# The input columns of a token pair: three full transposes and a stacked remainder, in place of doubled columns

## The chip, the cores and the metric

One core of a Trainium2 chip runs the kernel. The metric is device time in microseconds (us) of one execution; lower is better. Five engines work side by side, each through its own queue in order: TensorE (PE), VectorE (DVE), ScalarE (ACT), GpSimd (POOL) and SyncE (SP), which here issues nearly all transfers.

## What is computed

Each of 33280 tokens has 192 features in 8 heads. A softmax over 7 taps per head weighs the token's own and six earlier rows; the weighted sum is the input of a layer with 1024 hidden units.

```python
    w = exp(weight_gen - max); w = w / (sum(w) + 1e-09)
    out = np.einsum('bshk,bskhg->bshg', w, x_unf)      # 7 taps
    ...
    h = x @ w_in                                        # 192 -> 1024
    e = np.exp(h - h_max)
    solu = h * e / (sum(e) + 1e-09)
    ln = (solu - mu) / np.sqrt(var + 1e-06) * g_ln
    return (ln @ w_out).astype(np.float32)              # 1024 -> 192
```

## The kernel before

A tile is 128 tokens, one on each partition; there are 260 tiles, worked in pairs and in groups of four. Chunks of 4, 8 and then 16 tiles are loaded together (x in four transfers, the weights of the taps in one).

POOL forms the products of a group of four with the taps (L178) and adds them down to three terms (L446, L447, into `half`, two buffers). Before the first group of a chunk it scales the taps (L158 subtracts the maximum, L172 multiplies by the reciprocal that DVE makes at L170). DVE adds the three terms for two tiles at a time (`last_sum`, L464) into `a`. There each tile has 256 columns: its 192, and the last 64 a second time, copied by ACT once per group (`copy_columns`, L468). The first four tiles (`whole`) skip the additions on POOL: PE sums their seven products while it transposes, and DVE sums only the last 64 columns.

For a pair PE transposes four blocks of 128 columns in f32 into one PSUM tile `pa`, the only one of its kind (`transpose_x`, L486): for each tile columns 0 to 127, and columns 128 to 191 doubled. ACT copies `pa` to f16 (`high_x`, L494). PE subtracts that copy from `pa` with `minus` (`subtract_high`, L501, two matmuls of 256 columns; the second leaves the upper 64 rows of the doubled block whole), and ACT copies what is left (`low_x`, L508). So `x_lo[:, 1]` holds the high part of the last 64 features on 64 partitions and the low part on the other 64.

The first product of a tile (`first_product`, L522, here mm1) takes ten matmuls of 512 columns: high times `wa_hi` and `wa_lo`, low times `wa_hi`, and the stacked block times `wb_hi` and `wb_lo`, where `wb` has the last 64 rows of w_in twice. It writes one of three PSUM tiles `h`. DVE takes the maximum (L537), ACT the exponential (L544), DVE the product (L550), ACT the squares (L557) and the high f16 half (L564), DVE the low half (L568). When L557 and L568 of a tile are done, its `h` is free for the tile three later. SP transposes both halves by a transfer (L576), and PE forms the second product (L617, here mm2, 24 matmuls of 192 columns), six tiles behind mm1. ACT scales it (L628), and SP stores four tiles at once (L632).

The order on every engine is not written out. `plan` lists each step with a busy time, what it waits for and slack; `issue_order` walks that list and picks, on the engine that is free first, the step with the lowest key, made of the tile number and a number per step in `URGENCY`, among those that are ready within `PATIENCE`.

Of the kernel before, what the change touches and what calls it, by code (L numbers as in the profile page):

```python
# [27 lines left out]
def tile_kernel(ctx: ExitStack, tc: tile.TileContext, x, weight_gen, w_in, w_out, g_ln, out):  # L28
# [11 lines left out]
    TG = 4  # L40
    TC = 16

    starts = [0, TG, TG + TC // 2, *range(TG + TC, RUN + 1, TC)]
# [180 lines left out]
    minus = const.tile([P, 2, P], F16, name="minus")  # L224
    nc.vector.tensor_scalar_mul(minus[:, 0], ident, -1.0)
    nc.vector.tensor_scalar_mul(minus[:D2, 1], ident[:D2], 0.0)
    nc.vector.tensor_scalar_mul(minus[D2:, 1], ident[D2:], -1.0)
# [44 lines left out]
    wb_hi, wb_lo = wb[:, 0], wb[:, 1]  # L272
    wb_part = const.tile([P, 2, FH], F16, name="wb_part")

    def first_part(key, step):
# [17 lines left out]
        elif step == 8:  # L293
            for f in range(2):
                for k in range(2):
                    nc.sync.dma_start(
                        wb[k * D2 : (k + 1) * D2, :, f * FH : (f + 1) * FH],
                        wb_part[f * D2 : (f + 1) * D2],
                    )

    def weight_scale(step):
        if step == 0:
            total = first["total"] = ps_a.tile([P, 2, 2, P], F32, name="pa")[:, 0, 0, :1]
# [111 lines left out]
    def stat_group(t):  # L415

        n = 2 if t < 2 * TG else TG
        return n if t % n == n - 1 else 0


    def group(t):

        if t < TG:
            return 2 if t % 2 == 0 else 0
        return TG if t % TG == 0 else 0

    def whole(t):

        return t < TG

# [23 lines left out]
    def last_sum(t):  # L454
        if t % TG == 0:

            a_of[t // TG] = att.tile([P, TG, 2 * P], F32, name="a", bufs=3)
        at = t % TG
        if whole(t):
            out = columns(t, 2)[:, :, P:D]  # L460
            rows = pr_of[t][:, :, at : at + 2, P:].rearrange("p k t d -> p t d k")
        else:
            out, rows = columns(t, 2)[:, :, :D], half_of[t // TG * TG][:, at : at + 2]
        nc.vector.tensor_reduce(out, rows, axis=AX.X, op=ALU.add)  # L464

    def copy_columns(t):
        a = columns(t, group(t))
        nc.scalar.copy(a[:, :, D:], a[:, :, P:D])  # L468
# [4 lines left out]
    def transpose_x(t):  # L473
        a = a_of[t // TG]
        pa = ps_a.tile([P, 2, 2, P], F32, name="pa")

        rows = []
        for i in range(2):
            at = (t + i) % TG
            if whole(t):  # L480
                rows += [(0, i, pr_of[t][:, k, at, :P]) for k in range(K)]
            else:
                rows.append((0, i, a[:, at, :P]))
            rows.append((1, i, a[:, at, P:]))
        for k, (n, i, row) in enumerate(rows):
            nc.tensor.matmul(  # L486
                pa[:, n, i, :], row, ident, is_transpose=True,
                start=k == 0, stop=k == len(rows) - 1, skip_group_check=True,
            )
        x_parts[t] = [pa]  # L490

    def high_x(t):
        hi = small.tile([P, 2, 2, P], F16, name="x_hi", bufs=2)
        nc.scalar.copy(hi, x_parts[t][0])  # L494
        x_parts[t].append(hi)

    def subtract_high(t):

        pa, hi = x_parts[t]
        for n in range(2):  # L500
            nc.tensor.matmul(  # L501
                pa[:, n], minus[:, n], hi[:, n], start=False, stop=n == 1, skip_group_check=True
            )

    def low_x(t):
        pa, hi = x_parts.pop(t)
        lo = small.tile([P, 2, 2, P], F16, name="x_lo", bufs=2)
        nc.scalar.copy(lo, pa)  # L508
        for i in range(2):
            xt_of[t + i] = hi[:, :, i, :], lo[:, :, i, :]  # L510

    def first_product(t):
        hi, lo = xt_of.pop(t)
        h = ps_h.tile([P, FF], F32, name="h")
        halves = [slice(f * FH, (f + 1) * FH) for f in range(2)]
        terms = (
            (hi[:, 0, :], wa_hi), (hi[:, 0, :], wa_lo), (lo[:, 0, :], wa_hi),
            (lo[:, 1, :], wb_hi), (lo[:, 1, :], wb_lo),
        )
        for n, (lhs, rhs) in enumerate(terms):  # L520
            for fs in halves:
# [4 lines left out]

# [113 lines left out]
    def at_chunk(op, *args):  # L640
# [3 lines left out]
        att=attend, fin=last_sum, dup=copy_columns, xT=transpose_x, xhi=high_x, xn=subtract_high,  # L644
        xlo=low_x, mm1=first_product,
# [3 lines left out]
    for n in range(9):  # L649
# [27 lines left out]
    for op, t in issue_order(plan(RUN, starts, group, stat_group, whole, LOADS)):  # L677
# [3 lines left out]

URGENCY = {
# [290 lines left out]
```

## Time and profile before

| | |
|---|---|
| median of 3 runs | 1254.52 us (1254.21 to 1255.18) |
| span of the profiled execution | 1253.1 us; its own time is given only as this span |
| busy PE / DVE / ACT / POOL | 1190.3 / 1192.0 / 1198.0 / 1130.5 us |
| granted TensorE clock, mean | 0.995 |
| DMA, mean busy share of 16 engines in the steady part | 0.82 to 0.83 |

The span runs from the first to the last instruction; the median is 1.4 us above it. Busy times can overlap within an engine, as one instruction begins before the last has drained; how long one really holds its engine is read from the start of it to the start of the next. Idle time in the list of waits is put down to what ended it.

### The profile page before, as it was taken

Reading aid. Unit: us, or ns where it says so; the run is one execution under the profiler, and the core shown is the slowest. Engines: PE = TensorE matmul, PEld = TensorE weight load, DVE = VectorE, ACT = ScalarE, POOL = GpSimd, SP = SyncE. Lnnn points to the kernel's source line nnn. Section 1 sums busy time; section 2 is a strip of 40 time slices with the busy share of each in tenths; the row PEclk is TensorE's granted clock in tenths of the full one; section 3 lists DMA queues with packets and bytes.
Section 4 is the critical chain, followed back from the end, with each engine's and each line's share of the span. In section 5 each row is a group of like instructions: output and inputs, shape, how many; then the busy total and the mean of one; then the engine's idle time right before and its main releaser. Section 6 shows DMA issues by size and latency. Waiting matters only on the chain.

```text
span 1253.1 us, 25748 instructions
## 1 busy us (share of the span) xinstructions
PE 1190.3 (95%) x9666; PEld 862.2 (69%) x9666; DVE 1192.0 (95%) x1824; ACT 1198.0 (96%) x2389; POOL 1130.5 (90%) x236
## 2 busy tenths in 40 slices
PE   2687999999999999999999999999999999999997
PEld 2454777777677777777777777777777777777776
DVE  6879999999999999999999999999999999999984
ACT  5879999999999999999999999999999999999995
POOL 4998999999999999999999999999999999999800
PEclk9899999999999999999999999999999999999999
DMA  6387689695878869696987869699786979666654
GB/s 211 92 194 185 127 176 198 143 211 146 190 155 183 188 161 197 138 222 140 181 176 176 182 141 230 143 173 178 174 184 142 220 144 199 145 143 144 131 144 122
DMA packets 565885, 210.83 MB, mean 168 GB/s; under 512 B 544520, under 2 KB 546568, under 8 KB 565632
## 3 DMA queue, kind: packets, MB, share of 16 engines
q1 hardware_dynamic: 565352, 207.86, 76.6%
q8 instruction: 76, 1.25, 0.4%
q10 hardware_dynamic: 408, 1.33, 0.3%
q14 instruction: 49, 0.40, 0.1%
HBM read 46.55 MB, written 25.56 MB: 58 GB/s over the span
## 4 chain that ended last, share of the span: by engine, by line
ACT 49%; DVE 33%; issue 12%; PE 3%; DMA 2%; POOL 0%; ACTq 0%; SPq 0%; DVEq 0%; POOLq 0%
ACT e L557 12%; ACT hl L564 11%; ACT e L544 11%; DVE h L550 10%; DVE hl L568 9%; DVE h L537 8%; DVE a L464 4%; ACT ot L628 3%; ACT junk L114 3%; ACT x_hi L494 3%; ACT x_lo L508 2%; DMA xt<-in_x_dram 2%; PE h L522 1%; ACT stats L592 1%; DVE wy L170 1%
## 5 line engine op out<-in xcount | busy, mean ns | idle before, releaser
L178 POOL TENSOR_TENSOR pr<-xt,wt 128x5376 f32<-128x5376 f32 (+1 forms) x66 | 631.0, 9561 | 5.4 <-PE pa L486 1.5
L617 PEld LDWEIGHTS <-hlT 128*128 128x128 f16 x6240 | 523.4, 98 | 64.2 <-issue 19.6
L617 PE MATMUL po<-w_hl,hlT 128*128 128x192 f16 x6192 | 554.1, 246 | 8.1 <-ACT ot L628 8.1
L537 DVE TENSOR_SCALAR_CACHE_REDUCE h<-h,scal 128x1024 f32<-128x1024 f32 x260 | 334.2, 1285 | 6.3 <-PE h L522 5.9
L550 DVE SCALAR_TENSOR_TENSOR h<-h,scal,e 128x1024 f32<-128x1024 f32 x260 | 333.6, 1284 | 6.3 <-ACT e L544 6.3
L568 DVE SCALAR_TENSOR_TENSOR hl<-h,hl 128x1024 f16<-128x1024 f32 x260 | 316.0, 1216 | 18.7 <-ACT hl L564 13.3
L447 POOL TENSOR_TENSOR half<-pr 128x2304 f32<-128x2304 f32 x64 | 326.5, 5102 | 5.0
L544 ACT ACTIVATE e<-h,stats 128x1024 f32<-128x1024 f32 x260 | 292.5, 1125 | 6.2 <-DVE h L537 4.9
L557 ACT ACTIVATE e<-h,stats 128x1024 f32<-128x1024 f32 x260 | 291.9, 1123 | 1.9 <-DVE hl L568 0.7
L522 PE MATMUL h<-wa,x_hi 128*128 128x512 f16 x1040 | 268.4, 381 | 23.2 <-ACT e L557 17.7
L522 PEld LDWEIGHTS <-x_lo 128*128 128x128 f16 x1560 | 153.0, 98 | 186.2 <-issue 3.3
L564 ACT ACTIVATE hl<-h 128x1024 f16<-128x1024 f32 x260 | 268.6, 1034 | 11.5 <-DVE h L550 7.0
L522 PE MATMUL h<-wb,x_lo 128*128 128x512 f16 x1040 | 268.6, 381 | 0.0
L464 DVE TENSOR_REDUCE a<-half 128x384 f32<-128x1152 f32 x128 | 172.0, 1344 | 0.0
L522 PEld LDWEIGHTS <-x_hi 128*128 128x128 f16 x1040 | 101.0, 98 | 95.8 <-issue 23.6
L522 PE MATMUL h<-wa,x_lo 128*128 128x512 f16 x520 | 155.6, 381 | 0.0
L446 POOL TENSOR_TENSOR pr<-pr 128x768 f32<-128x768 f32 x64 | 116.1, 1815 | 5.0
L628 ACT ACTIVATE ot<-po,stats 128x192 f32<-128x192 f32 x258 | 111.1, 430 | 7.8 <-PE po L617 7.8
L486 PE MATMUL pa<-ident,a 128*128 128x128 f32 x516 | 79.1, 275 | 1.1 <-ACT a L468 1.1
L508 ACT CAST x_lo<-pa 128x512 f16<-128x512 f32 x130 | 78.0, 600 | 1.4 <-PE pa L501 1.2
L494 ACT CAST x_hi<-pa 128x512 f16<-128x512 f32 x130 | 75.6, 582 | 1.3 <-PE pa L486 1.3
L486 PEld LDWEIGHTS pa<-ident,a 128*128 128x128 f32 x516 | 59.3, 142 | 7.9 <-ACT a L468 1.7
(88 smaller groups left out, 693.6 us busy)
## 6 DMA issues: line engine op xcount, KB each, us to landing
out_dram<-ot SPq DMA_DIRECT2D x65, 384.0 KB, 3.0
xt<-in_x_dram SPq DMA_DIRECT2D x30, 576.0 KB, 4.8
xt<-in_x_dram SPq DMA_DIRECT2D x30, 480.0 KB, 4.4
wt<-in_weight_gen_dram SPq DMA_DIRECT2D x15, 448.0 KB, 5.0
hlT<-hl SPq DMA_TRANSPOSE x260, 3.8
raw<-in_moe_w_out_dram SPq DMA_DIRECT2D x2, 768.0 KB, 10.0
xt<-in_x_dram SPq DMA_DIRECT2D x3, 384.0 KB, 5.6
xt<-in_x_dram SPq DMA_DIRECT2D x1, 1152.0 KB, 7.9
```

The costliest lines, as they stand in the source:

```text
L178: nc.gpsimd.tensor_tensor(out=window(pr, at * D, [(TG * D, K), (HG, n * H), (1, HG)]), in0=window(xt, t * D, [(D, K), (HG, n * H), (1, HG) ...
L447: nc.gpsimd.tensor_tensor(out=half.rearrange("p t d j -> p j t d"), in0=pr[:, :3], in1=pr[:, 3:6], op=ALU.add)
L464: nc.vector.tensor_reduce(out, rows, axis=AX.X, op=ALU.add)
L522: nc.tensor.matmul(h[:, fs], lhs, rhs[:, fs], start=n == 0, stop=n == len(terms) - 1)
L537: nc.vector.tensor_scalar(h, h, scal_of(chunk_of(t), HS), None, op0=ALU.mult, op1=ALU.min, accum_out=stat(t, NMAX),)
L544: nc.scalar.activation(e, h_of[t], AF.Exp, bias=stat(t, NMAX), scale=-1.0, accum_out=stat(t, Z))
L550: nc.vector.scalar_tensor_tensor(out=h, in0=h, scalar=scal_of(chunk_of(t), NSIG), in1=e, op0=ALU.mult, op1=ALU.mult, accum_out=stat(t, M),)
L557: nc.scalar.activation(e_of.pop(t), h_of[t], AF.Square, bias=stat(t, M), scale=-float(FF), accum_out=stat(t, Q),)
L564: nc.scalar.activation(hl[:, 0, :], h_of[t], AF.Copy, scale=2.0**15)
L568: nc.vector.scalar_tensor_tensor(out=hl[:, 1, :], in0=h_of[t], scalar=2.0**15, in1=hl[:, 0, :], op0=ALU.mult, op1=ALU.subtract,)
L617: nc.tensor.matmul(po[:, :D], hlT[:, half * NJ + j, :], w2_hl[:, j, w, :], start=n == 0, stop=n == len(terms) - 1,)
L628: nc.scalar.activation(ot[:, t % TG, :], po[:, :D], AF.Copy, scale=stat(t, OUT))
```

## The change

The three doubled things go: the copy of the last 64 columns, the fourth transpose and the second subtracting matmul. The 384 columns of a pair lie side by side and are transposed as three blocks of 128. Block 0 holds columns 0 to 127 of the even tile; block 1 holds columns 128 to 191 of the even tile on partitions 0 to 63 and columns 0 to 63 of the odd tile on partitions 64 to 127; block 2 holds columns 64 to 191 of the odd tile. The stacked blocks are made afterwards by three transfers from SBUF to SBUF for each pair, of 64 partitions by 128 f16 (256 bytes a row) each: one after the high copy (`move_high`), two after the low one (`move_low`). The ten matmuls of mm1 keep their sizes, but the even tile uses `wa` and `w2x`, the odd tile `wb` and `w0x`, four arrangements of w_in built at the start by nine transfers in place of four.

The buffers change too: `x_hi` and `x_lo` three in place of two, the tap weights `wt` two in place of three. In the first four tiles PE transposes 21 product blocks a pair (seven products in three blocks) in place of 14 and two of summed columns and DVE sums nothing. `URGENCY` and `PATIENCE` are new, and keys may differ for even and odd tiles.

```diff
-        wt = ws[c] = io.tile([P, TC * HK], F32, name="wt", bufs=3)
+        wt = ws[c] = io.tile([P, TC * HK], F32, name="wt", bufs=2)
...
+        elif step >= 8 and key == "a":
+            nc.sync.dma_start(wb[:D2], wa[D2:])
+            for to in (w0x[:D2], w0x[D2:]):
+                nc.sync.dma_start(to, wa[:D2])
+        elif step >= 8:
+            for to in (w2x[:D2], w2x[D2:]) if step == 8 else (wb[D2:],):
+                for f in range(2):
                     nc.sync.dma_start(
...
-    def copy_columns(t):
-        a = columns(t, group(t))
-        nc.scalar.copy(a[:, :, D:], a[:, :, P:D])
...
         if whole(t):
+            sources = [(pr_of[t], k * TG * D + at) for k in range(K)]
         else:
+            sources = [(a_of[t // TG], at)]
+        rows = [(n, window(a, first + n * P, [(1, P)])) for n in range(3) for a, first in sources]
...
+        hi = small.tile([P, 4, P], F16, name="x_hi", bufs=X_BUFS)
+        nc.scalar.copy(hi[:, :3], x_parts[t][0])
...
+    def move_high(t):
+        hi = xt_of[t][0]
+        nc.sync.dma_start(hi[D2:, 3], hi[D2:, 1])
...
-        for n in range(2):
-            nc.tensor.matmul(
-                pa[:, n], minus[:, n], hi[:, n], start=False, stop=n == 1, skip_group_check=True
-            )
+        nc.tensor.matmul(pa, minus, hi[:, :3], start=False, stop=True, skip_group_check=True)
...
+    def move_low(t):
+        hi, lo = xt_of[t]
+        nc.sync.dma_start(hi[D2:, 1], lo[:D2, 1])
+        nc.sync.dma_start(hi[:D2, 3], lo[D2:, 1])
...
+        w, w_rest = (wb, w0x) if odd else (wa, w2x)
+        whole_x, rest = hi[:, 2 * odd], hi[:, 2 * odd + 1]
         terms = (
+            (whole_x, w[:, 0]), (whole_x, w[:, 1]), (lo[:, 2 * odd], w[:, 0]),
+            (rest, w_rest[:, 0]), (rest, w_rest[:, 1]),
         )
...
-            add("lw", t, SP, 60, 0, last_group(c - 3), dma=1270)
+            add("lw", t, SP, 60, 0, last_group(c - 2), dma=1270)
...
-PATIENCE = (9, 56, 153, 18, 1.40474e+28)
+PATIENCE = (149.784, 111.565, 53.9239, 19.6637, 1651.94)
```

The new keys move instructions on every engine. Three places follow.

DVE before, in the middle of the program. L537 is the maximum of a tile (mm1 has to be done), L550 the product, L568 the low half that frees an `h`; the number behind `h` names its tile, in the order 7457, 7520, 7575, 7630.

```order
L568 SCALAR_TENSOR_TENSOR hl_7573<-h_7457,hl_7573 128x1024
L537 TENSOR_SCALAR h_7575,stats_134<-h_7575,scal_79 128x1024
L550 SCALAR_TENSOR_TENSOR h_7520,stats_134<-h_7520,scal_79,e_7588 128x1024
L588 TENSOR_REDUCE stats_134<-stats_134 128x4
L156 TENSOR_REDUCE wm_7642<-wt_6447 128x128
L550 SCALAR_TENSOR_TENSOR h_7575,stats_134<-h_7575,scal_79,e_7623 128x1024
L568 SCALAR_TENSOR_TENSOR hl_7645<-h_7520,hl_7645 128x1024
L588 TENSOR_REDUCE stats_134<-stats_134 128x4
L537 TENSOR_SCALAR h_7630,stats_134<-h_7630,scal_79 128x1024
```

Between the low half that frees an `h` (of 7457) and the maximum of the tile that takes it (7630) stand five long instructions here; over tiles 20 to 249 there are four, five or six, and never fewer.

DVE after, at about the same tile. L518 is the maximum, L531 the product, L549 the low half; the tiles are 7541, 7593, 7650, 7718.

```order
L518 TENSOR_SCALAR h_7650,stats_134<-h_7650,scal_79 128x1024
L569 TENSOR_REDUCE stats_134<-stats_134 128x4
L549 SCALAR_TENSOR_TENSOR hl_7663<-h_7541,hl_7663 128x1024
L549 SCALAR_TENSOR_TENSOR hl_7707<-h_7593,hl_7707 128x1024
L531 SCALAR_TENSOR_TENSOR h_7650,stats_134<-h_7650,scal_79,e_7715 128x1024
L569 TENSOR_REDUCE stats_134<-stats_134 128x4
L518 TENSOR_SCALAR h_7718,stats_134<-h_7718,scal_79 128x1024
```

The maximum of 7718 now stands two long instructions behind the low half of 7541; over tiles 20 to 249 that number is 2 for 52 tiles, 3 for 42, and 4 to 7 for the other 136.

POOL before, around the first group of a chunk: L172 and L158 are the scaling steps of the taps (L158 works for the next chunk), L178, L446 and L447 a group.

```order
L172 TENSOR_TENSOR wt<-wt,wy 128x896
L178 TENSOR_TENSOR pr<-xt,wt 128x5376
L446 TENSOR_TENSOR pr<-pr 128x768
L447 TENSOR_TENSOR half<-pr 128x3x768
L158 TENSOR_TENSOR wt<-wt,wm 128x896
```

POOL after, at the end of a chunk: L155 and L169 are the same two steps, L175, L429 and L430 a group.

```order
L155 TENSOR_TENSOR wt<-wt,wm 128x896
L175 TENSOR_TENSOR pr<-xt,wt 128x5376
L429 TENSOR_TENSOR pr<-pr 128x768
L430 TENSOR_TENSOR half<-pr 128x3x768
L169 TENSOR_TENSOR wt<-wt,wy 128x896
```

The first step of the next chunk's taps has moved from behind the first group of a chunk to ahead of its last; one group, no longer three, lies between it and the second step. On DVE the reciprocal that the second step reads has moved too: it stood one maximum ahead of the sums of the chunk's last group, and stands two maxima ahead.

SP after, where a chunk is loaded: L473, L488 and L489 are the three small transfers, L557 the transpose, L84 and L73 the loads, L613 the store. Before, only transposes, loads and stores stood here.

```order
L473 DMA x_hi_7403<-x_hi_7403 64x128
L557 DMA_TRANSPOSE hlT_7422<-hl_7366 128x16x128
L84 DMA wt_7424<-in_weight_gen_dram 128x896
L73 DMA xt_7426<-in_x_dram 128x960
L488 DMA x_hi_7403<-x_lo_7429 64x128
L489 DMA x_hi_7403<-x_lo_7429 64x128
L557 DMA_TRANSPOSE hlT_7491<-hl_7432 128x16x128
L613 DMA out_0_dram<-ot_7312 128x768
```

Three transfers a pair have come in between the transposes, 390 in all, and each waits on SP for the copy on ACT that makes its source.

## Rows read from the trace of the kernel before

**Rows 1.** The page: the chain that ended last, by engine.

```profile
ACT 49%; DVE 33%; issue 12%; PE 3%; DMA 2%; POOL 0%; ACTq 0%; SPq 0%; DVEq 0%; POOLq 0%
```

**Rows 2.** Busy us by stretch: PE, PEld, DVE, ACT, POOL; clock, DMA share, GB/s.

```profile
300.00:600.00 300.00, 297.63 (x2449) 216.38 (x2448) 295.75 (x455) 298.03 (x592) 291.85 (x58) 1.00 0.82 174
600.00:900.00 300.00, 298.18 (x2446) 216.10 (x2445) 295.90 (x450) 297.87 (x593) 287.57 (x60) 1.00 0.83 173
```

**Rows 3.** Waits from 100 to 1100 us: total us, times, longest us.

```profile
POOL wt L172 <- DVE wy L170: 19.9, 11, 2.9
...
DVE hl L568 <- ACT hl L564: 12.3, 51, 0.5
PE h L522 <- ACT e L557: 10.2, 17, 1.8
...
PE h L522 <- DVE hl L568: 1.9, 1, 1.9
```

**Rows 4.** Timeline of POOL (start us, us, instruction, [idle before]), seven chunks apart.

```profile
609.60 1.76 POOL L172 TENSOR_TENSOR wt<-wt,wy 128x896 f32<-128x896 f32 x1 [1.77 <-DVE wy L170]
...
1117.50 1.76 POOL L172 TENSOR_TENSOR wt<-wt,wy 128x896 f32<-128x896 f32 x1 [1.75 <-DVE wy L170]
```

**Rows 5.** Timeline of PE, the steady part.

```profile
603.91 0.60 PE L486 MATMUL pa<-ident,a 128*128 128x128 f32 x4
604.35 1.03 PE L522 MATMUL h<-wa,x_hi 128*128 128x512 f16 x4
...
606.51 2.14 PE L617 MATMUL po<-w_hl,hlT 128*128 128x192 f16 x24
608.49 1.03 PE L522 MATMUL h<-wa,x_hi 128*128 128x512 f16 x4
...
612.62 0.38 PE L501 MATMUL pa<-x_hi,minus 128*128 128x256 f16 x2
612.84 1.03 PE L522 MATMUL h<-wa,x_hi 128*128 128x512 f16 x4
```

**Rows 6.** Timeline of ACT, the same part.

```profile
601.52 0.43 ACT L468 COPY a<-a 128x256 f32<-128x256 f32 x1
601.82 0.62 ACT L508 CAST x_lo<-pa 128x512 f16<-128x512 f32 x1
602.29 0.44 ACT L592 ACTIVATE stats<-stats,scal 128x4 f32<-128x4 f32 x1
...
603.86 1.06 ACT L564 ACTIVATE hl<-h 128x1024 f16<-128x1024 f32 x1
604.78 1.15 ACT L544 ACTIVATE e<-h,stats 128x1024 f32<-128x1024 f32 x1
```

**Rows 7.** Timeline of DVE, the same part.

```profile
601.01 1.21 DVE L568 SCALAR_TENSOR_TENSOR hl<-h,hl 128x1024 f16<-128x1024 f32 x1
602.14 1.28 DVE L550 SCALAR_TENSOR_TENSOR h<-h,scal,e 128x1024 f32<-128x1024 f32 x1
603.34 1.29 DVE L537 TENSOR_SCALAR_CACHE_REDUCE h<-h,scal 128x1024 f32<-128x1024 f32 x1
```

**Rows 8.** Transfers: KB each and median us to landing; issue ns; landing min/median/max of L576.

```profile
wt<-in_weight_gen_dram SPq DMA_DIRECT2D x15, 448.0 KB, 5.0
...
wb<-wb_part SPq DMA_DIRECT2D x4, 128.0 KB, 2.4
...
L296 SPq DMA_DIRECT2D wb<-wb_part x4: 605/606/682, 27.3 to 29.3; - x4
...
DMA to landing us min/median/max: 3.6/3.8/9.7
```

**Rows 9.** Timeline of the start: DVE, PE, POOL.

```profile
21.97 1.70 DVE L464 TENSOR_REDUCE a<-pr 128x128 f32<-128x896 f32 x1 [0.81 <-POOL pr L178]
...
23.49 1.73 PE L486 MATMUL pa<-ident,pr 128*128 128x128 f32 x7 [0.44 <-ACT w_scale L307]
...
32.85 9.70 POOL L178 TENSOR_TENSOR pr<-xt,wt 128x5376 f32<-128x5376 f32 x1 [1.51 <-PE pa L486]
```

More of the change, by code (lines that the diff above doesn't have):

```diff
@@ L39, in tile_kernel @@
     PB = P // B
-    TG = 4
-    TC = 16
-    starts = [0, TG, TG + TC // 2, *range(TG + TC, RUN + 1, TC)]
+    starts = chunk_starts(RUN)
     NCHUNK = len(starts) - 1
@@ L223, in tile_kernel @@
     nc.vector.memset(norms[:, 0], 0.0)
[L224 to L227, printed above, removed]
+    minus = const.tile([P, P], F16, name="minus")
+    nc.vector.tensor_scalar_mul(minus, ident, -1.0)
     scratch = {}
@@ L302, in weight_scale @@
         if step == 0:
-            total = first["total"] = ps_a.tile([P, 2, 2, P], F32, name="pa")[:, 0, 0, :1]
+            total = first["total"] = ps_a.tile([P, 3, P], F32, name="pa")[:, 0, :1]
             for k in range(2):
@@ L413, in tile_kernel @@
     o_of = {}
[L415 to L429, printed above, removed]
     pr_of = {}
@@ L455, in last_sum @@
         if t % TG == 0:
-            a_of[t // TG] = att.tile([P, TG, 2 * P], F32, name="a", bufs=3)
+            a_of[t // TG] = att.tile([P, TG, D], F32, name="a", bufs=3)
         at = t % TG
[L459 to L464, printed above, removed]
-    def copy_columns(t):
-        a = columns(t, group(t))
-        nc.scalar.copy(a[:, :, D:], a[:, :, P:D])
+        nc.vector.tensor_reduce(
+            columns(t, 2), half_of[t // TG * TG][:, at : at + 2], axis=AX.X, op=ALU.add
+        )
     x_parts = {}
     def transpose_x(t):
[L474 to L485, printed above, removed]
+        pa = ps_a.tile([P, 3, P], F32, name="pa")
+        at = t % TG * D
+        if whole(t):
+            sources = [(pr_of[t], k * TG * D + at) for k in range(K)]
+        else:
+            sources = [(a_of[t // TG], at)]
+        rows = [(n, window(a, first + n * P, [(1, P)])) for n in range(3) for a, first in sources]
+        for k, (n, row) in enumerate(rows):
             nc.tensor.matmul(
-                pa[:, n, i, :], row, ident, is_transpose=True,
+                pa[:, n, :], row, ident, is_transpose=True,
                 start=k == 0, stop=k == len(rows) - 1, skip_group_check=True,
@@ L648, in tile_kernel @@
     )
-    for n in range(9):
+    for n in range(10):
         for key in "ab":
@@ L676, in tile_kernel, with chunk_starts, stat_group, group @@
     ctx.enter_context(tc.manual_schedule())
-    for op, t in issue_order(plan(RUN, starts, group, stat_group, whole, LOADS)):
+    for op, t in issue_order(plan(RUN, starts, LOADS)):
         ops[op](t)
-URGENCY = {
[16 rows of a table removed]
+TG = 4
+TC = 16
+def chunk_starts(run):
+    return [0, TG, TG + TC // 2, *range(TG + TC, run + 1, TC)]
+def stat_group(t):
+    n = 2 if t < 2 * TG else TG
+    return n if t % n == n - 1 else 0
+def group(t):
+    if t < TG:
+        return 2 if t % 2 == 0 else 0
+    return TG if t % TG == 0 else 0
+def whole(t):
+    return t < TG
+URGENCY = {
[15 rows of a table added]
 }
-PATIENCE = (9, 56, 153, 18, 1.40474e+28)
+PATIENCE = (149.784, 111.565, 53.9239, 19.6637, 1651.94)
 PE, DVE, ACT, SP, POOL = range(5)
 TRANSPOSE, COPY = 1, 2
-def plan(run, starts, group, stat_group, whole, loads):
+PARITY = True
+def plan(run, starts, loads):
     hop = {
@@ L753, in plan @@
     once("b8", SP, 1800, "b7", dma=600)
+    once("a8", SP, 1350, "a7", "b8", dma=1000)
+    once("b9", SP, 900, "b7", "b8", dma=300)
     for f in "01":
@@ L805, in plan @@
             g = groups[i - 2]
-            after.append(("fin", g + group(g) - 2))
-            if whole(g):
-                after.append(("xT", g))
+            after.append(("xT", g) if whole(g) else ("fin", g + group(g) - 2))
         if i and whole(groups[i - 1]) and not whole(t):
-            after += [("fin", groups[i - 1]), ("xT", groups[i - 1])]
+            after.append(("xT", groups[i - 1]))
         if c > 1:
```

57 lines of the change are left out of this document (27 added, 30 removed), and 31 rows, old and new, of the table URGENCY.

## Prediction

> **What bounds the kernel now.** Read the chain of waits first [rows 1]: ACT and DVE carry it by turns, 49% and 33%, so no single engine holds the whole path. Then read busy time by stretch [rows 2]. In 600 us of the steady part PE is busy 595.81, ACT 595.90, DVE 591.65 and POOL 579.42: idle 0.7%, 0.7%, 1.4% and 3.4%. Four engines are nearly full at once, and relief of one is worth at most what the next has left.
>
> The pace comes from POOL's scaling steps [rows 4]: 1117.50 − 609.60 = 507.90 us for seven chunks, 72.56 us for 16 tiles, **9.07 us for a pair**. POOL is not the limit: each time it stands there 1.75 to 1.77 us, waiting for the reciprocal that comes through DVE.
>
> The waits [rows 3] say what DVE lacks. It is idle 8.35 us in 600 [rows 2], 0.126 us a pair, and of those 13.9 us in a thousand 12.3 are waits for the high half on ACT, in 51 pieces of at most 0.5 us. PE waits for an `h` to come free, mostly from ACT's squares (10.2 us in 17 pieces, 0.6 each) and once from DVE's low half. So in the steady part ACT is the engine that comes late, and DVE is next.
>
> **The change part by part.**
>
> *ACT, removed.* The copy of doubled columns holds ACT from 601.52 to 601.82, 0.30 us for two pairs, 0.15 a pair. The two copies of `pa` shrink from 512 to 384 columns: 512 columns hold ACT 0.47 us (601.82 to 602.29), 1024 columns 0.92 (603.86 to 604.78), so 0.88 ns a column, and 128 fewer save 0.11 us in each copy [rows 6]. Together 0.15 + 0.22 = 0.37 us a pair, 48 us of ACT work in 130 pairs. It does not all turn into time: it only pulls ACT out of the way of DVE and PE.
>
> *PE, removed.* Four transposes hold PE from 603.91 to 604.35, 0.11 us each; one goes. The subtracting pair of 256 columns holds it from 612.62 to 612.84; one matmul of 384 columns is three quarters of that, 0.055 us less [rows 5]. Together 0.165 us a pair, 21 us in all, of PE's own work. mm1 and mm2 stay as they are.
>
> The Trainium skill ("TensorE: Matmul & The Clock Gate", section "Part 4: PE-mode transpose") gives about 275 ns for one 128 by 128 transpose within a kernel. By that price PE would lose 36 us of transposes where the starts above give 14; the sum would be the same, since PE isn't what comes late, only PE's lead at the tight places below would be larger. The measured interval decides here, as transposes overlap one another.
>
> *DVE, unchanged in the steady part.* It still makes the sums, maxima, products and low halves. So DVE sets the best case: with every wait gone a pair takes 9.07 − 0.126 = 8.94 us, and over the 1130 us from about 100 to 1230 the gain is at most 0.014 × 1130 = 15.7 us. POOL allows it: without its wait a chunk is 72.56 − 1.77 = 70.8 us, 8.85 a pair. **I take the waits for ACT's high half as gone**, 12.3 us in 1000, so **−13.9 us** (bounds 0 and −15.7), since 0.37 us of relief a pair is three times the 0.11 us that they cost. POOL's wait shrinks too, because the reciprocal has moved one maximum ahead on DVE; that only lets POOL follow.
>
> *The new order on DVE, added risk.* mm1 of a tile needs the `h` that the low half of the tile three before frees, and the maximum needs mm1. mm1 holds PE 604.35 to 606.51, 2.16 us [rows 5]. Before, at least four long instructions stood between (about 4.7 us at 1.13 and 1.20 each [rows 7]), so mm1 had over 2 us of play, more than the mm2 that may be under way on PE (606.51 to 608.49, 1.98 us). In the changed order 52 of 230 tiles have only two, a low half and a product, say: 1.13 + 1.20 = 2.33 us, against 2.16 and the way there and back. There is no play: unless PE is already waiting when the low half ends, DVE stops, and behind it on its queue stand the low halves and products of other tiles, which ACT and SP wait for. Over 260 tiles that is 59 places. Each costs between 0 (PE is early, and it has 0.165 us a pair more lead) and 1.98 us (an mm2 has just begun). The nearest rows are the 0.6 us pieces in which PE waits for `h`, with ample play. I take 0.07 us, near the lower end because PE has the lead, so **+4 us**. This is the weakest term.
>
> *SP and the small transfers.* 390 transfers of 64 partitions come onto SP's queue. The nearest row is the building of `wb`, 605 ns to issue and 2.4 us to land [rows 8]. Two issues and a landing are 3.6 us. The cover: by the order on ACT and PE, after the low copy of a pair at least mm1, mm2, mm1, mm2 of earlier tiles and six of ten matmuls of its own mm1 run before the stacked block is read, 2 × 4.14 + 1.3 = 9.6 us. So I cost them at **nothing**, bounded below by nothing too, as they free no engine. Queued behind them on SP are transposes; their reader mm2 now stands seven tiles behind mm1, no longer six, so one tile of slack, 4.5 us, has been added there. If the cover fails, see the third rival.
>
> The Trainium skill ("DMA: Bandwidth & Descriptors", section "Specifications") wants at least 512 bytes a transfer for full rate and says that smaller ones are read, modified and written. These rows have 256 bytes. By that rule the transfers land later than the row of 1024-byte pieces says; the sum stays while they land inside the cover, and the rule raises only the chance of the third rival.
>
> The weights of the taps lose a buffer, so their load waits for the same group as the loads of x. It lands in 5.0 us [rows 8]; its first reader on DVE stands about two tiles (9 us) behind it. Nothing, for that reason.
>
> *The start.* Seven transposes of the first tiles take 1.73 us, 0.24 each [rows 9]; 21 in place of 16 are 1.2 us more for each of two pairs, and POOL's third product begins only when the second pair is read (it waits 1.51 us for that already). Five more transfers build w_in, 3.0 us of issue at 605 ns [rows 8], ahead of the second tile's mm1. On the other side DVE drops two sums of 1.70 us, and ACT two copies. Bounds −3.4 and +6 (2.4 + 3.0, rounded up); I take **+1.5**, since POOL has its waits to give back later. The end keeps eight mm2 behind the last mm1, as before: nothing.
>
> **Sum** against the profiled span: 1253.1 − 13.9 + 4 + 1.5 = 1244.7 us; with the 1.4 us that the median lies above it, **1246 us**.
>
> **The rivals.**
>
> *One: the gain is used up.* DVE has the same 8.94 us of work whatever ACT does. If the tight places cost 0.2 us each, 59 × 0.2 = 12 us, the sum is 1254.5 − 13.9 + 12 + 1.5 = **1254 us**. For it: DVE's margin is only 1.4%. Against: nearly all of that margin is ACT's lateness.
>
> *Two: slower, through the ring of three `h`.* At a tight place PE is in the middle of an mm2 and DVE stops for what is left of it. At the 0.6 us of the nearest row the price is 59 × 0.6 = 35 us: 1254.5 − 13.9 + 35.4 + 1.5 = **1278 us**. It decides above (13.9 − 1.5) / 59 = 0.21 us a place. For it: PE keeps 98% of its work, so it is seldom idle when a low half ends. Against: PE's new lead of 0.165 us a pair is 0.37 us for each tight place, about two pairs apart.
>
> *Three: slower, through late small transfers.* Where a chunk is loaded, one pair's low transfers stand behind two loads. With two issues (1.2 us) and the worst landing of a transpose, 9.7 us [rows 8], the block comes at 10.9 us against 9.6 us of cover, and each issue ahead of it adds 0.6: 2.5 us with two loads. On 15 chunks that is 37 us, and **1283 us**; from 8.5 / 15 = 0.57 us a chunk the gain is gone. For it: a transfer behind a transpose in a ring whose engines are 0.82 busy [rows 2]. Against: the median landing of the nearest copy is 2.4 us.
>
> *Four: a larger gain.* All of DVE's idle time goes, the tight places cost nothing and the start wins 3.4 us: 1254.5 − 15.7 − 3.4 = **1235 us**.
>
> **How the numbers follow.** Forecast (1238 to 1252 around 1246) 0.55; rival one 0.16; rival two 0.15; rival three 0.07; rival four 0.07. A measurement of this kernel tells 0.2%, 2.5 us, from no change. Faster (under 1252) is the forecast and rival four, 0.62; within 0.2% is rival one, 0.16; slower is two and three, 0.22. The range goes from 1234, below the best case, to 1264, which takes in the cheaper half of rival two (0.37 us a place), and leaves out about 0.15.
>
> **What the profile of the changed kernel would show.** If the steps are right: a period of POOL's second scaling step of about 71.6 to 72.0 us; DVE at 99% or more and ACT near 95% in the steady part; no wait of DVE for ACT's high half worth naming; copies of `pa` starting 0.36 us before what follows them. If rival one or two is right: DVE waits for PE at the maximum, total over 10 us. If rival three is right: PE waits for `x_hi` from a transfer at mm1, in pieces near the chunks. If the start went wrong: POOL's third product well behind 32.85 us [rows 9] with the shorter period afterwards. The prediction would be wrong as a whole if ACT still came late, that is if the waits for the high half stayed although ACT has idle time.

## The result, and the profile after

The changed kernel takes **1273.05 us** (median of four runs, 1269.90 to 1273.90) against 1254.55 for the kernel before on the same chip: ratio **1.0146**, 95% interval 1.0132 to 1.0160. It is slower by 18.5 us, where 1246 was forecast, and outside the range. The profiled execution has a span of 1271.6 us. One execution of `short_lead_old`, below, fell in a far slower state and is left out of its median.

The page after, busy time and the chain (beside [rows 1]):

```profile
PE 1179.9 (93%) x9418; PEld 839.3 (66%) x9418; DVE 1194.3 (94%) x1820; ACT 1153.1 (91%) x2323; POOL 1130.2 (89%) x236
...
DVE 30%; ACT 29%; issue 18%; PE 14%; DMA 8%; SPq 1%; ACTq 0%; DVEq 0%
```

The work did shrink as reckoned: ACT was busy 1198.0 us before and is busy 1153.1 now, 45 us less against the 48 of the prediction. The time grew all the same, so the engines stand more. By stretch (columns as in [rows 2]):

```profile
300.00:600.00 300.00, 287.04 (x2300) 203.64 (x2299) 288.32 (x436) 277.50 (x557) 282.86 (x58) 0.99 0.80 174
600.00:900.00 300.00, 294.54 (x2381) 210.19 (x2380) 297.11 (x451) 286.45 (x579) 289.32 (x59) 1.00 0.80 178
```

Between 600 and 900 DVE is at 99.0%, as forecast. Between 300 and 600 it is at 96.1%: all engines lose there, 7 us on DVE alone. The waits from 100 to 1100 us (total us, times, longest us) name who is late:

```profile
POOL wt L169 <- DVE wy L167: 28.7, 11, 6.8
...
PE h L504 <- DVE hl L549: 18.6, 26, 2.9
ACT junk L111 <- DMA xt<-in_x_dram: 16.3, 11, 3.3
...
DVE hl L549 <- ACT hl L545: 10.5, 7, 2.8
...
DVE h L518 <- PE h L504: 3.8, 13, 1.2
```

New is ACT's wait for loads of x, 16.3 us at L111, the sums of squares of a chunk, which stood among no larger wait before. DVE's waits for PE, the sign of rival two, are 3.8 us. PE's waits for a transfer at mm1, the sign of rival three, are not among the larger ones. DVE's wait for ACT's high half, which the prediction took as gone, is 10.5 us, while ACT is idle 22.5 us between 300 and 600: the sign by which the prediction would be wrong as a whole.

Where the time went is seen from when each tile's exponential starts (worked out from ACT's rows L544 and L525), as the lag behind the kernel before, in us:

| tile | 8 | 16 | 24 | 48 | 64 | 88 | 128 | 200 | 256 |
|---|---|---|---|---|---|---|---|---|---|
| changed kernel | −7.5 | +12.2 | +6.4 | +7.2 | +12.9 | +18.0 | +17.7 | +21.4 | +18.7 |
| no_moves | −9.5 | +6.1 | +0.3 | −0.7 | +1.7 | +3.6 | +1.5 | +3.2 | −0.2 |
| loads_early_20 | −7.3 | +5.9 | +1.6 | −0.4 | +2.0 | +2.8 | +0.2 | −0.4 | −3.5 |

Some 6 us are lost by tile 24, 11 more between tiles 48 and 88, and from there on the pace is that of before, while loads_early_20 gains 6 us on it. The two lower rows are experiments, below.

At the start PE stands once for a transposed half (its row, then the stretch behind that wait, columns as in [rows 2]):

```profile
97.22 4.02 PE L598 MATMUL po<-w_hl,hlT 128*128 128x192 f16 x24 [4.51 <-DMA hlT<-hl]
```

```profile
96.00:101.00 5.00, 3.78 (x24) 3.60 (x25) 2.98 (x5) 0.86 (x2) 4.84 (x3) 0.50 0.60 109
```

PE had stood idle since 92.7. The granted clock of this stretch is 0.50, 1.2 GHz where 2.4 is full, and this mm2 takes 4.02 us; at full clock one takes 2.14.

### The profile page after: what moved, and what is told of

It is laid out like the page before. It is cut to its first block, busy times and chain, and to the rows that moved or that the text cites. A ratio compares the mean times of both kernels' runs of the same rounds, so it can differ in the third digit from the quotient of the medians.

```text
span 1271.6 us, 26132 instructions
## 1 busy us (share of the span) xinstructions
PE 1179.9 (93%) x9418; PEld 839.3 (66%) x9418; DVE 1194.3 (94%) x1820; ACT 1153.1 (91%) x2323; POOL 1130.2 (89%) x236
## 3 DMA queue, kind: packets, MB, share of 16 engines
q1 hardware_dynamic: 597080, 215.32, 75.6%
## 4 chain that ended last, share of the span: by engine, by line
DVE 30%; ACT 29%; issue 18%; PE 14%; DMA 8%; SPq 1%; ACTq 0%; DVEq 0%
DVE h L531 8%; DVE hl L549 8%; ACT e L525 8%; PE h L504 7%; ACT e L538 6%; DVE h L518 6%; ACT hl L545 6%; PE po L598 5%; DVE a L441 4%; DMA xt<-in_x_dram 4%; ACT ot L609 2%; ACT junk L111 2%; DMA hlT<-hl 2%; ACT x_hi L467 1%; ACT x_lo L483 1%
## 5 line engine op out<-in xcount | busy, mean ns | idle before, releaser
L175 POOL TENSOR_TENSOR pr<-xt,wt 128x5376 f32<-128x5376 f32 (+1 forms) x66 | 630.9, 9559 | 4.6 <-PE pa L457 0.8
L504 PEld LDWEIGHTS <-x_hi 128*128 128x128 f16 x2080 | 201.3, 98 | 249.9 <-issue 47.2
L531 DVE SCALAR_TENSOR_TENSOR h<-h,scal,e 128x1024 f32<-128x1024 f32 x260 | 333.3, 1287 | 10.5 <-ACT e L525 9.1
L518 DVE TENSOR_SCALAR_CACHE_REDUCE h<-h,scal 128x1024 f32<-128x1024 f32 x260 | 334.8, 1288 | 8.3 <-PE h L504 7.0
L549 DVE SCALAR_TENSOR_TENSOR hl<-h,hl 128x1024 f16<-128x1024 f32 x260 | 313.3, 1219 | 22.7 <-ACT e L538 10.7
L430 POOL TENSOR_TENSOR half<-pr 128x2304 f32<-128x2304 f32 x64 | 326.3, 5099 | 5.0
L525 ACT ACTIVATE e<-h,stats 128x1024 f32<-128x1024 f32 x260 | 294.5, 1133 | 6.5 <-DVE h L518 6.1
L504 PE MATMUL h<-wb,x_hi 128*128 128x512 f16 x520 | 133.9, 380 | 23.1 <-DVE hl L549 16.5
L504 PE MATMUL h<-wa,x_hi 128*128 128x512 f16 x520 | 134.7, 381 | 8.7 <-ACT e L538 3.3
L504 PE MATMUL h<-w2x,x_hi 128*128 128x512 f16 x520 | 134.7, 382 | 0.7 <-DMA x_hi<-x_lo 0.7
L504 PE MATMUL h<-w0x,x_hi 128*128 128x512 f16 x520 | 133.4, 379 | 0.8 <-DMA w0x<-wa 0.8
L429 POOL TENSOR_TENSOR pr<-pr 128x768 f32<-128x768 f32 x64 | 116.1, 1815 | 5.0
L504 PEld LDWEIGHTS <-x_lo 128*128 128x128 f16 x520 | 51.0, 98 | 62.1 <-issue 1.1
L504 PE MATMUL h<-wa,x_lo 128*128 128x512 f16 x260 | 78.3, 383 | 0.0
L504 PE MATMUL h<-wb,x_lo 128*128 128x512 f16 x260 | 77.3, 379 | 0.0
L169 POOL TENSOR_TENSOR wt<-wt,wy 128x896 f32<-128x896 f32 (+2 forms) x18 | 28.9, 1603 | 52.7 <-DVE wy L167 44.4
```

The costliest lines, as they stand in the source:

```text
L175: nc.gpsimd.tensor_tensor(out=window(pr, at * D, [(TG * D, K), (HG, n * H), (1, HG)]), in0=window(xt, t * D, [(D, K), (HG, n * H), (1, HG) ...
L430: nc.gpsimd.tensor_tensor(out=half.rearrange("p t d j -> p j t d"), in0=pr[:, :3], in1=pr[:, 3:6], op=ALU.add)
L504: nc.tensor.matmul(h[:, fs], lhs, rhs[:, fs], start=n == 0, stop=n == len(terms) - 1)
L518: nc.vector.tensor_scalar(h, h, scal_of(chunk_of(t), HS), None, op0=ALU.mult, op1=ALU.min, accum_out=stat(t, NMAX),)
L525: nc.scalar.activation(e, h_of[t], AF.Exp, bias=stat(t, NMAX), scale=-1.0, accum_out=stat(t, Z))
L531: nc.vector.scalar_tensor_tensor(out=h, in0=h, scalar=scal_of(chunk_of(t), NSIG), in1=e, op0=ALU.mult, op1=ALU.mult, accum_out=stat(t, M),)
```

## The experiments

First the parts of the change one by one. All times are medians; a ratio is to the kernel before on the same chip, with its 95% interval.

| run | us | ratio | interval |
|---|---|---|---|
| relief_old_order | 1248.97 | 0.9950 | 0.9935 to 0.9964 |
| new_layout_old_order | 1289.56 | 1.0280 | 1.0249 to 1.0312 |
| old_layout_new_order | 1344.17 | 1.0713 | 1.0695 to 1.0730 |
| no_moves | 1254.70 | 1.0000 | 0.9990 to 1.0010 |
| moves_unread | 1271.68 | 1.0138 | 1.0121 to 1.0155 |
| moves_no_wait | 1267.52 | 1.0107 | 1.0065 to 1.0148 |
| norms_later | 1283.04 | 1.0229 | 1.0213 to 1.0244 |
| lead_old_order | 1300.74 | 1.0372 | 1.0357 to 1.0388 |
| norms_together | 1286.94 | 1.0265 | 1.0248 to 1.0282 |
| loads_early | 1256.76 | 1.0023 | 1.0013 to 1.0033 |
| act_high | 1284.02 | 1.0241 | 1.0226 to 1.0257 |
| unread_old_order | 1252.13 | 0.9991 | 0.9981 to 1.0000 |
| **loads_early_20** | **1250.52** | **0.9975** | 0.9963 to 0.9988 |
| no_moves_loads_early | 1248.39 | 0.9957 | 0.9941 to 0.9972 |
| before_loads_early | 1254.02 | 0.9996 | 0.9987 to 1.0006 |
| short_lead_old | 1276.16 | 1.0183 | 1.0160 to 1.0205 |
| loads_half_early | 1261.71 | 1.0054 | 1.0039 to 1.0069 |
| loads_earlier_20 | 1262.82 | 1.0067 | 1.0049 to 1.0084 |

### The relief, the order and the transfers apart

**relief_old_order** is the kernel before without the doubled columns:

```
-            pa[:, n], minus[:, n], hi[:, n], ...      (two matmuls of 256)
+            flat[0], minus[:, 0], flat[1], ...        (one of 384)
-        nc.scalar.copy(hi, x_parts[t][0])
+        nc.scalar.copy(window_(hi), window_(x_parts[t][0]))   # 384 columns
```

> The kernel before with its own order, and only the relief of the change from tile 4 on: no doubled columns, three transposes for a pair, one subtracting matmul of 384 columns, copies of 384 columns, and no small transfers (what would stand in the stacked block is left out, so the product of the last 64 columns is not the right one; the matmuls keep their number and size). If the step of the prediction holds that ACT's lateness is what DVE waits for, about 1240 us (1238 to 1245). If DVE has the same work and nothing to gain, 1252 to 1255. If the old order can't use the room, 1255 or more.

Measured about 6 us faster, not 14. Its waits from 100 to 1100 us, and its stretches:

```profile
PE h L535 <- ACT e L570: 12.6, 19, 2.0
...
ACT hl L577 <- DVE h L563: 7.2, 12, 0.8
...
DVE h L563 <- ACT e L557: 5.3, 24, 0.3
DVE hl L581 <- ACT hl L577: 2.9, 15, 0.3
```

```profile
300.00:600.00 300.00, 296.28 (x2400) 210.81 (x2399) 297.07 (x455) 292.06 (x579) 294.35 (x60) 1.00 0.80 173
600.00:900.00 300.00, 296.53 (x2389) 209.94 (x2388) 296.58 (x455) 291.68 (x579) 288.97 (x59) 1.00 0.82 178
```

DVE's wait for the high half did fall, from 12.3 us [rows 3] to 2.9. But DVE gained only 2.0 us of work in 600 (593.65 against 591.65 [rows 2]): it now waits for the exponentials, 5.3 us in 24 pieces. ACT gained idle time and waits for DVE. A wait that is removed between two engines that feed each other came back, in part, at the next hand-over.

**new_layout_old_order** keeps the transfers but the row order of before, **old_layout_new_order** the reverse:

```
-    for op, t in issue_order(plan(RUN, starts, LOADS)):
+    for op, t in old_order(RUN, starts, LOADS):       # xmh behind xhi, xml behind xlo
```

> The changed kernel with the order of the kernel before: its list of steps, without the copy of doubled columns and the early sums, each small transfer right behind the copy that makes its source, the load of the tap weights moved ahead of the loads of x of its chunk. If the new order is what costs, 1240 to 1249 us. If the small transfers or the three that stand on SP in every pair cost, whatever the order, 1262 us or more.

> The kernel before with the order of the changed kernel: its list of steps without the small transfers, the copy of doubled columns made once for each pair (0.05 us a pair more on ACT than before), three x_hi and x_lo, two tap weights. If the new order is what costs, 1275 us or more, since ACT and PE have no relief here. If the small transfers cost, 1262 us or less.

Neither part stands alone: 1289.56 and 1344.17. In the first, the transfers land too late for mm1, which the old order issues earlier behind them. Its waits from 100 to 1100 us:

```profile
PEld L504 <- DMA x_hi<-x_lo: 45.6, 26, 4.4
POOL wt L169 <- DVE wy L167: 36.8, 12, 8.2
PE h L504 <- DMA x_hi<-x_lo: 33.5, 23, 4.0
```

In the second, ACT's copy of the doubled columns, which the new order has no place for, was put right ahead of each pair's transposes, and PE waits for it there:

```profile
PE pa L486 <- ACT a L468: 51.6, 69, 1.7
```

So this run shows the price of that place, and not of the new order by itself.

**no_moves** is the changed kernel without the 390 small transfers:

```
-        nc.sync.dma_start(hi[D2:, 3], hi[D2:, 1])
-        nc.sync.dma_start(hi[D2:, 1], lo[:D2, 1])
-        nc.sync.dma_start(hi[:D2, 3], lo[D2:, 1])
```

> The changed kernel in its own order without its 390 small transfers (the stacked block of both tiles is then an unfinished one, so the product of the last 64 columns is not the right one; all matmuls stay). If the new order is what costs, 1268 to 1274 us, as after. If the transfers, or the waits that they bring onto SP, cost, 1245 to 1256 us.

1254.70: the transfers cost **18.4 us**, the whole loss. What is left of the change is worth nothing, though in the old order the same relief gave about 6. ACT's wait for the x loads is smaller, but still there (100 to 1100 us):

```profile
ACT junk L111 <- DMA xt<-in_x_dram: 5.7, 4, 2.6
```

### How the transfers cost: the landing, the waits or the issues

**moves_unread** sends them to a tile that nothing reads; **moves_no_wait** also reads a constant, so that they wait for no copy:

```
+        sc = small.tile([P, 2, P], F16, name="x_sc", bufs=X_BUFS)
-        nc.sync.dma_start(hi[D2:, 3], hi[D2:, 1])
+        nc.sync.dma_start(sc[D2:, 1], hi[D2:, 1])     # moves_no_wait: minus[D2:]
```

> The changed kernel with its 390 small transfers at the same places of SP's row and behind the same copies of ACT, but written to a tile of their own that nothing reads; the product takes the rows from where no_moves takes them (one of two tiles with wrong rows). The theory that the transfers cost by what they do to SP's row (they stand ahead of the transposes and the x loads and wait there for ACT) expects 1268 to 1275, the changed kernel's own time. The rival, that PE waits for them to land, expects 1254 to 1257, the time without them. Between these the cost is split.

> As moves_unread, but the transfers read a constant tile, so that none of them waits for ACT; their issues (0.47 us each) and their places in SP's row stay. If the waits at the head of SP's row are the cost, 1254 to 1259; if it is the issues themselves and what the transfers take of the DMA rings, 1266 to 1275. Rows of the product are wrong in one of two tiles, as there.

Unread, they cost as much (1271.68), so it isn't the landing. Without the waits for ACT 1267.52: the start comes back (tile 24 lags 0.0, in no_moves 0.3), the rest does not. From tile 24 to 256 its profile loses 12.3 us, as much as the changed kernel, and ACT's wait for the x loads stays:

```profile
ACT junk L111 <- DMA xt<-in_x_dram: 17.3, 10, 3.5
```

So most of it is that they stand in SP's row at all. The four times of this run spread from 1261.19 to 1274.74, so the share of the waits is not settled by it.

**unread_old_order** does the same to new_layout_old_order, **lead_old_order** and **short_lead_old** start each pair's chain a whole pair, or 14 places, earlier there (the last with `X_BUFS = 4`):

```
+            keyed.append((max(i - by, fins[t]) + 0.5, i, (name, t)))     # short_lead_old
```

> new_layout_old_order (1289.6) with its transfers written to a tile that nothing reads, as in moves_unread; one of two tiles has wrong rows. With the old order PE waited 33.5 us for their landing. If the landing is what they cost there, 1250 to 1262; if SP's row is, as with the new order, 1280 to 1290; if both, in between.

> new_layout_old_order (1289.6) with each pair's transposes, copies and transfers one pair earlier from the pair of tile 22 on, all else in its order. There the transfers landed after the product was due (23 waits of 4.0 us on PE). If that lateness alone made the 20 us that it lost behind tile 20, those go and it gives 1268 to 1273, with no wait of PE for x_hi left; if the transfers cost as much by SP's row, 1280 to 1290.

> new_layout_old_order (1289.6) with each pair's transposes, copies and transfers 14 places (some 0.8 of a tile) earlier from tile 8 on and a fourth buffer for the pair's halves; with a whole pair and three buffers ACT waited 23.2 us for a free one and it took 1300.7. If the late landing is what the transfers cost in the old order, 1252 to 1262; if the earlier chain costs as much elsewhere (PE waiting for the sums), 1270 to 1300.

In the old order the cost is another one: unread, 1252.13, so 37 of its 40.6 us above relief_old_order were the landing, and only 3 are left for SP's row, the start and the buffers. More lead did not settle it. A whole pair turned it into waits of ACT for a free `x_hi` (23.2 us) and of PE's transposes for DVE (24.3 us); 14 places took back 13 us, with 14.8 us of loads of PE's weights and 9.5 of its matmuls still waiting for `x_hi`. None of the three leads tried here fits both the chain and the landing into the old order.

### The loads of x

In SP's row of the changed kernel (start us, us, queue, line) the third and fourth load of a chunk stand behind transposes that wait for DVE, and among the small transfers; below it ACT's row:

```profile
334.02 0.57 SPq L73 DMA_DIRECT2D xt<-in_x_dram  x1
...
336.47 0.59 SPq L73 DMA_DIRECT2D xt<-in_x_dram  x1
337.16 8.86 SPq L557 DMA_TRANSPOSE hlT<-hl  x2
346.13 0.53 SPq L488 DMA_DIRECT2D x_hi<-x_lo  x1
346.71 0.59 SPq L489 DMA_DIRECT2D x_hi<-x_lo  x1
347.35 0.58 SPq L73 DMA_DIRECT2D xt<-in_x_dram  x1
348.03 0.46 SPq L473 DMA_DIRECT2D x_hi<-x_hi  x1
348.54 3.15 SPq L557 DMA_TRANSPOSE hlT<-hl  x1
351.73 0.57 SPq L73 DMA_DIRECT2D xt<-in_x_dram  x1
```

```profile
355.98 1.06 ACT L111 ACTIVATE junk<-xt 128x1024 bf16<-128x1024 f32 x1 [3.34 <-DMA xt<-in_x_dram]
```

ACT is ready for the first square 0.9 us after the fourth load was issued (355.98 − 3.34 − 351.73). In the kernel before the fourth load of this chunk was issued at 339.25 and its first square ran at 352.05, 12.8 us later:

```profile
339.25 0.58 SPq L76 DMA_DIRECT2D xt<-in_x_dram  x1
```

```profile
352.05 1.11 ACT L114 ACTIVATE junk<-xt 128x1024 bf16<-128x1024 f32 x1
```

The orders say the same: between them stand 12 long instructions of ACT in most chunks of before, 3 in the changed order (and 7 in loads_early_20, below). The new order spent that slack, and the transfers push the loads back: over the 15 long chunks the fourth load goes out 18.5 us behind the first in the mean, in no_moves 17.4. The loads land no later than before (4.5 us at the median between 100 and 1100 us, before 4.7), so it is their place in SP's row that is late and not the DMA engines. `plan`, which made the order, reckons 60 ns of SP for such an issue, where these rows show 0.46 to 0.59 us; whether it spent the slack for that reason was not tried.

In this chunk the wait went further. PE stands for the high copy that ACT makes behind its squares:

```profile
359.95 0.32 PE L478 MATMUL pa<-x_hi,minus 128*128 128x384 f16 x1 [2.95 <-ACT x_hi L467]
360.11 3.04 PE L598 MATMUL po<-w_hl,hlT 128*128 128x192 f16 x24
```

The granted clock from 361.3 to 364.5 us is 0.50 (1.2 GHz), and the mm2 takes 3.04 us instead of 2.14.

**norms_later** and **norms_together** move the squares instead of the loads, by 34 places of the issue order (17 to 18 places are a tile), or to the last of the three:

```
+    if name in ("s0", "s1") and t >= 36:
+        keyed.append((at["s2", t] - 0.5, i, (name, t)))
```

> The changed kernel with the sums of squares of each chunk's x (and the eight small steps behind them) 34 places later in the order from the chunk of tile 36 on, two tiles behind where they stood. Tiles 56 to 88 lost 8 us against the kernel before, and there ACT stands at such a step for a load that SP issued late. If that wait is the loss, the time falls by 6 to 10, to 1263 to 1267, and ACT's wait for the x load (16.3 us between 100 and 1100) falls below 4. If the load's lateness only shows a lateness that all steps share, the time stays at 1271 to 1275.

> The changed kernel with the first two of a chunk's three sums of squares put right in front of the third on ACT, from the chunk of tile 36 on, and nothing else moved. They wait 16.3 us in all for the x load between 100 and 1100, 10.6 more than without the transfers. If the transfers cost by making the loads late for ACT there, 1262 to 1266; if that wait only shows a lateness that comes another way, 1271 to 1275.

Both took ACT's wait away and were 10 and 14 us *slower*. In norms_together the reason shows (waits from 100 to 1100 us):

```profile
DVE scal L119 <- ACT junk L111: 22.2, 14, 2.2
```

DVE's sum of these norms stands right behind the last square in its row; two squares more ahead of it, and DVE, the fuller engine, waits once a chunk. In norms_later DVE waits 20.7 us for ACT's squares `e` and POOL 34.0 for DVE; why the shift brings that stays open.

**loads_early** leaves the squares and issues the last three loads of a chunk 18 places (about a tile) earlier, from the chunk of tile 36 on; **loads_early_20** from the chunk of tile 20 on:

```
+        if name in ("lx1", "lx2", "lx3") and t >= first:
+            keyed.append((max(at["lx0", t] + 0.5, i - 18), i, (name, t)))
```

> The changed kernel with the last three x loads of each chunk about one tile earlier in SP's row (the second right behind the first). Late loads as the way the transfers cost: 1262 to 1267, and ACT's wait for the loads (16.3 us) mostly gone. If what is late are the transposes behind the small transfers, the loads now stand ahead of more of them, and it gives 1272 to 1280.

> loads_early with the x loads of the chunk of tile 20 moved too. loads_early still lost 12.6 us by tile 16 and kept 6.8 of it at tile 24; there ACT waits 3.0 us for an x load and PE 4.8 us for a transpose behind it. If late loads are the cause there too, the time falls by 3 to 7, to 1250 to 1254; if the transposes are late by themselves, it stays at 1255 to 1259.

1256.76 and **1250.52**, the fastest version with all of the computation: 22.5 us below the changed kernel and 0.25% below the kernel before. The same place in loads_early_20, SP and ACT:

```profile
326.31 0.58 SPq L73 DMA_DIRECT2D xt<-in_x_dram  x1
...
327.40 0.43 SPq L73 DMA_DIRECT2D xt<-in_x_dram  x1
...
329.05 0.60 SPq L73 DMA_DIRECT2D xt<-in_x_dram  x1
329.74 8.15 SPq L557 DMA_TRANSPOSE hlT<-hl  x2
...
339.22 0.59 SPq L73 DMA_DIRECT2D xt<-in_x_dram  x1
```

```profile
345.12 1.05 ACT L111 ACTIVATE junk<-xt 128x1024 bf16<-128x1024 f32 x1
```

The third load now passes the long transposes, the fourth is issued 5.9 us ahead of the square, and no wait stands before it. The stretches, and the waits from 100 to 1100 us:

```profile
300.00:600.00 300.00, 293.79 (x2385) 209.96 (x2384) 297.31 (x455) 285.70 (x574) 294.07 (x60) 1.00 0.83 180
600.00:900.00 300.00, 295.34 (x2394) 211.14 (x2392) 298.39 (x456) 287.73 (x578) 289.53 (x59) 1.00 0.79 178
```

```profile
ACT hl L545 <- DVE stats L569: 18.7, 20, 2.5
PE h L504 <- DVE hl L549: 17.7, 27, 2.9
...
DVE hl L549 <- ACT hl L545: 1.1, 2, 0.8
```

DVE is at 99.1 and 99.5%, and its waits for ACT's high half are down to 1.1 us. PE still waits for the low halves 27 times, 26 in the changed kernel; with DVE that full there is little for these waits to cost. SP itself still stands for ACT's high copies nearly as long as in the changed kernel (changed kernel, then loads_early_20):

```profile
SPq L473 <- ACT x_hi L467: 97.6, 40, 4.4
```

```profile
SPq L473 <- ACT x_hi L467: 81.5, 38, 3.6
```

So these waits cost through what stands behind them in the row, and little once the loads stand ahead.

Is this the transfers' cost that goes, or a gain of its own?

> no_moves (1254.7) with the same early loads; the 390 small transfers are left out, so one of two tiles has wrong rows. If early loads only undo what the transfers did, 1252 to 1255, as no_moves; if loads were late there too (ACT waited 5.7 us for them), 1246 to 1251, and the transfers still cost what loads_early_20 stands above it.

> The kernel before with the same early loads. No wait for an x load stands among its larger ones. If early loads mend what the changed kernel spoiled, 1253 to 1256; if they are a gain of their own that any version would have, 1245 to 1251.

| us | loads as placed | 18 places earlier |
|---|---|---|
| kernel before | 1254.55 | 1254.02 |
| changed, without the transfers | 1254.70 | 1248.39 |
| changed | 1273.05 | 1250.52 |

The kernel before has nothing to gain from it. In the new order the loads were late by themselves (6.3 us), and the transfers cost 2.1 us when the loads have their lead and 18.4 when they don't. How much lead:

> loads_early_20 (1250.5) with half the lead, 9 places instead of 18. If the loads' lateness against ACT's squares is the cost, some of the wait of 16.3 us comes back: 1254 to 1264, between the changed kernel (1273) and the full lead. If any move from the old places mends it, 1249 to 1253.

> loads_early_20 with a lead of 30 places. With 18, ACT's wait for loads is gone from the larger waits and DVE works 99% of the time between 300 and 900, so nothing is left to win there: 1248 to 1252. If loads closer together hold up the transposes of the same queue, 1253 to 1262.

0, 9, 18 and 30 places give 1273.05, 1261.71, 1250.52 and 1262.82. Half the lead gives half the gain, so the size of the lead decides. Too much loses again, and more than half of that in the start: of the 8.9 us between the two profiled spans (1258.3 and 1249.4) 6.8 stand at tile 16, which lags 12.7 us against 5.9, and 5.2 at tile 24. There the transposes are late for mm2 (PE's row in loads_earlier_20, then in loads_early_20). Three loads go out in a row ahead of them, but the changed kernel has the same wait with its loads apart, so that this is the reason is not shown:

```profile
97.46 4.02 PE L598 MATMUL po<-w_hl,hlT 128*128 128x192 f16 x24 [4.37 <-DMA hlT<-hl]
```

```profile
93.97 2.15 PE L598 MATMUL po<-w_hl,hlT 128*128 128x192 f16 x24 [1.14 <-DMA hlT<-hl]
```

The granted clock from 96 to 101 us is 0.50 in the first and 1.00 in the second. Later PE waits for `x_hi` from a small transfer, 5.7 us in 8 pieces between 100 and 1100 us, where loads_early_20 has 0.8.

**act_high** has one of the three transfers made by ACT, as it stays on its partitions:

```
+        nc.scalar.copy(hi[D2:, 3], x_parts[t][0][D2:, 1])
-        nc.sync.dma_start(hi[D2:, 3], hi[D2:, 1])
```

> The changed kernel with one of a pair's three small transfers, the one between blocks on the same 64 partitions, made by a second copy of ACT of 64 rows by 128 columns (about 0.2 us, 130 times). SP loses 130 of its 390 issues and all its waits for x_hi (130 us in all). If the transfers cost by SP's row, a third of the 12.5 us of their issues and most of the 5.5 us of their waits go: 1262 to 1266. If ACT's 26 us of added work stand on the path, 1280 to 1295.

11 us slower, as expected if ACT's added work stands on the path. ACT's wait for the loads fell from 16.3 to 5.3 us, but ACT carries 23.9 us more work between 100 and 1100 (959.7 against 935.8), and DVE waits 9.7 us, 27 times, for its exponentials. An engine that is busy 94% of a stretch was no free place for 0.2 us a pair.

## Why the prediction was wrong, point by point

- **"SP and the small transfers: nothing"** is the step that failed: they cost 18.4 us. The cover that it named for mm1 held: mm1 does not wait for them in the changed order, and rival three, which let them land late, did not happen here (it did in the old order). What it left out is what else stands in SP's row. It named the load of the tap weights and its reader, and that held (DVE waits 0.7 us for it). It named the transposes and gave mm2 4.5 us more slack: that failed once, at the start, where mm2 waited 4.51 us for one. The loads of x and their reader, ACT's squares, it did not price. There the new order had cut the slack from 12 long instructions to 3, which the two orders showed without any run.
- **"The waits for ACT's high half as gone, −13.9"** had the mechanism right and was mis-sized. In the changed kernel the waits stayed (10.5 us), as ACT itself came late by the loads; with the loads early they went (1.1 us). But the relief alone gave about −6 in the old order, where DVE got only 2.0 us more work in 600, and at best, with loads early and no transfers, −6.2. There POOL's second scaling step shows the period, seven chunks apart:

```profile
604.64 1.76 POOL L169 TENSOR_TENSOR wt<-wt,wy 128x896 f32<-128x896 f32 x1 [1.19 <-DVE wy L167]
...
1108.50 1.75 POOL L169 TENSOR_TENSOR wt<-wt,wy 128x896 f32<-128x896 f32 x1 [1.23 <-DVE wy L167]
```

That is 71.98 us a chunk, inside the forecast 71.6 to 72.0 and 0.58 below before, where −13.9 over 1130 us asks for 0.89. The bound of −15.7 counted all of DVE's idle time as winnable.
- **"The new order on DVE, +4"**: the tight places show as PE waiting for DVE's low halves, 18.6 us, not as DVE waiting for PE (3.8 us). With the loads early the new order without transfers is as fast as the old (1248.39 and 1248.97), so the new order as a whole costs about nothing then; rival two fell, and rival one with it. That no_moves comes to rival one's 1254 is chance: its gain is used up by late loads (6.3 us), not at the tight places.
- **"The start, +1.5"**: +6.4 at tile 24, just above its upper bound of 6. PE's wait for a transposed half is 4.5 us there, 2.3 without the transfers and 1.9 in moves_no_wait and in loads_early_20. Taking away the transfers' waits for ACT brings 6.4 us of the lag back, moving the loads 4.8; both stand ahead of that transpose in SP's row.
- **ACT and PE, removed**: right in size on ACT, 45 of 48 us; of PE's 21 the page shows 10.

The terms as measured: −6.2 (relief, all loads in time), +6.3 (loads late by the new order), +2.1 (transfers, loads in time), +16.2 (transfers on top of late loads): 1254.6 + 18.4 = 1273.0. Each is good to about a microsecond, as the kernel before itself measured 1254.18 to 1255.21 beside these runs.

What stays open: norms_later's loss, how the transfers' cost is split between their waits and their issues, and whether some lead in the old order would fit the landing. The transfers from a queue other than SP's were not tried.

## What to carry to other kernels

A transfer that is put on a queue is priced by everything that stands behind it in that row, and by the reader of each of those, not only by its own reader. When a planner gives a new order, count for each load the long instructions between its issue and its first reader, before and after: slack that was never waited for appears in no list of waits. And when engines feed each other at 97 to 99%, removing one engine's lateness need not win all that the next has idle; here it won less than half (6.2 of 15.7 us).

## What was not expected of the hardware

The small transfers of 64 partitions by 256 bytes were cheap in themselves and dear in the row. From the page after (KB each, median us to landing):

```profile
x_hi<-x_lo SPq DMA_DIRECT2D x260, 16.0 KB, 2.1
...
x_hi<-x_hi SPq DMA_DIRECT2D x130, 16.0 KB, 2.2
```

They land in 2.1 to 2.2 us at the median and 6.5 at the worst, beside 2.4 for the `wb` pieces [rows 8], which have rows of 1024 bytes but are 128 KB in place of 16. The queue's share of the DMA engines went from 76.6 to 75.6% of a longer span, 960 and 961 us, so 390 transfers added next to nothing. A price of their short rows, which the prediction weighed, shows in neither; no run here has the same transfers with longer rows. What holds SP's row longest are its issues of transposes: 1.3 us at the least, 1.7 at the median and 5.7 at the most, 2 of them 8.86 us in the rows above, with their waits.
